# Banded attention and two gated MLPs on one core: VectorE and ScalarE put in written order beside TensorE

## The chip, the cores and the metric

The kernel runs on one core of one Trainium2 chip. The metric is the device time of one execution in microseconds (us); the median of three runs is quoted. One further execution was recorded by the hardware profiler, and every duration below comes from that one.

## What is computed

```python
# attention, for each of 4 sequences and 8 heads: 576 tokens, 64 wide, a window of 128
scores = q @ k.T / 8 + bias               # bias: -slope[h] * |i - j|, masked outside the window
attn = softmax(scores)
x = (attn @ v), heads side by side        # 2304 tokens x 512
# first gated MLP
x = (x @ w_a) * (x @ w_b) @ w_out         # inner width 1536
# second
out = ((x @ w1) * (x @ w2)) @ w3 @ w_out2 # inner width 1024
```

All arrays are float32. The large products are done as three products of a high and a low part in TensorE's fp32r type (`hi` is the rounded value, `lo` the rest).

## The kernel before

**The steps.** Each sequence has five blocks of query rows, four of 128 and one of 64. `RUNS` (line 34) puts them in runs of two, two and one; a step is one run of one pair of heads. Four pairs make 12 steps for a sequence and 48 for the whole, numbered 0 to 47 here; three more steps (`LAG`, line 35) drain the pipeline. `attention_ops` (line 642) yields the calls of each step, and the loop at line 716 makes them.

In step n TensorE does the scores of step n (`scores`, L309), the product with v of step n-3 (`pv`, L395), the transposition of one q or k block of the next run (`prep`, L273), then some work of the first gated MLP, and last the transposition of the probabilities of step n-1 (`probs`, L374). VectorE reduces the scores with their bias to row maxima (`step_exps`, L336), scales the exponentials of step n-1 (`norms`, L349 to L356), and makes the low parts: of the transposed q or k block (`parted`, L283), of the attention output (`pv_out`, L410). ScalarE does the exponentials (L342), the high parts (L282, L409) and most evictions of the transposed probabilities (L376). The small helpers `sub` and `evict` record their own lines, L72, L259 and L261.

**The gate work inside attention.** `Filler` (line 670) holds the work of the first two weight chunks, cut to tiles of 256 tokens: 54 items, each of 12 matmuls, each put down at 1.28 us by its planner. An item is half of a gate product (`g1`, L532) or half of an output product (`g2_two`, L560). At the `None` of every step, `run` is given `FILL` = 1.6 us to spend. An item may go only when its tokens have left attention (`ready`, set at line 412, where the last pair of heads of a run is done) and when the six weight parts are counted as whole.

**The first weights.** `Stages.turn` (line 158) is called once per step (twice in step 1). It moves each of up to three weight parts one stage on, the oldest first, and starts a new one. The stages of `convert` (line 97) turn 64-bit words into float32 and then into a high and a low part: `s0` on ScalarE (L107, L110), `s1` on VectorE (L114, L117, L121), `s3` an add (L126), and `split` (ScalarE makes the high part, L133; a subtraction makes the low part, L72). For the first six parts the add and the subtraction are on VectorE.

**What sets the order.** Line 715 fixes TensorE's order to the order of the program. VectorE's, ScalarE's, GpSimd's and SyncE's orders are chosen at build time by the tile framework from the program order, the dependencies and its own estimate of time. Each engine then runs its list strictly in that order.

**PSUM.** Eight banks: two for the MLP work (`ps_g`), three for scores (`ps_s`, line 182; a step takes two, or one in the short run), three for everything that is transposed and for `pv` (`ps_t`, line 183).

**Warm-up matmuls.** `keep_warm` (line 360) issues matmuls of 512 columns on a dummy tile that nothing reads. `pv` calls it in the first sequence, one after each full block (line 400).

After attention the rest of the gate items runs with more banks, and then the remaining groups of both MLPs (line 750), where TensorE is fed by 512-column matmuls.

Of the kernel before, what the change touches and what calls it, by code (L numbers as in the profile page):

```python
# [8 lines left out]
F32 = mybir.dt.float32  # L9
# [25 lines left out]
LAG = 3  # L35
PES, PTS = 4, 4
FILL = 1.6
PACE = (1.0, 1.0)
TURN = 400
WARM_RUNS, WARM = 3, 1  # L40
# [3 lines left out]
def attention_moe_moe(ctx, tc, q, k, v, w_a, w_b, w_o, w_1, w_2, w_3, w_o2, out):  # L44
# [137 lines left out]
    ps_s = asb.enter_context(tc.tile_pool(name="ps_s", bufs=3, space=PSUM))  # L182
    ps_t = asb.enter_context(tc.tile_pool(name="ps_t", bufs=3, space=PSUM))
# [79 lines left out]
    def prep(run, n):  # L263
# [11 lines left out]
        def parted():  # L275
            ps = hold[0]
            if x == 0 and m == LAST:
                dst = [(slice(j * D, (j + 1) * D), q_t2, slice(j * D, (j + 1) * D)) for j in range(2)]
            else:
                dst = [(slice(0, P), k_t if x else q_t, slice(i * P, i * P + m))]  # L280
            for o, (hi, lo), c in dst:
                nc.scalar.activation(hi[o, :, c], ps[o], ACTF.Copy)  # L282
                sub(nc.vector, lo[o, :, c], ps[o], f32(hi[o, :, c]))  # L283

        return trans, parted
# [30 lines left out]
    def exps(step):  # L316
        run = RUNS[step[1]]
        st = sm_p.tile([P, 4, 2 * len(run)], F32, name="st", bufs=4)
        at = 0
        for i in run:  # L320
            nj = window(i)[3]
            live[step, i]["st"] = st[:, :, at:at + nj]
            step_exps(step, i)
            at += nj
        live[step] = st[:, :, 0:at]

    def step_exps(step, i):
        hp = step[2]
        m, n, nb, nj = window(i)
        d = live[step, i]  # L330
        ps = d.pop("ps")
        pe = d["pe"] = sm_p.tile([P, 2, 2 * P], F32, name="pe", bufs=PES)
        st = d["st"]
        for j in range(nj):
            bias = relb[:, 2 * hp + j, 2 * P - n:] if nj == 2 else relb2[:, hp, :]
            nc.vector.tensor_tensor_reduce(  # L336
                out=pe[:, j, :n], in0=ps[j], in1=bias,
                scale=-1.0 / float(D) ** 0.5, scalar=3.0e38, op0=ALU.add, op1=ALU.min,
                accum_out=st[:, 0, j:j + 1],
            )  # L340
        for j in range(nj):
            nc.scalar.activation(  # L342
                pe[:, j, :n], pe[:, j, :n], ACTF.Exp, bias=st[:, 0, j:j + 1], scale=-1.0,
                accum_out=st[:, 1, j:j + 1],
            )
# [20 lines left out]
    def probs(step, i):  # L366
# [3 lines left out]
        ps = ps_t.tile([P, W], F32, name="tr")[:, 0:nj * n]  # L370
# [4 lines left out]
        t = d["pt"] = sm_p.tile([P, W], F32, name="pt", bufs=PTS)[:, 0:nj * n]  # L375
# [5 lines left out]
    def pv(step):  # L381
# [5 lines left out]
        for i in RUNS[rn]:  # L387
# [12 lines left out]
            if b == 0 and rn < WARM_RUNS and m == P:  # L400
                keep_warm(WARM, warm)

    def pv_out(step):
        b, rn, hp = step
        run = RUNS[rn]
        m = sum(window(i)[0] for i in run)
        o = slice(b * S + run[0] * P, b * S + run[0] * P + m)
        ps = outs.pop(step)[:, :m]
        nc.scalar.activation(x_hi[:, hp, o], ps, ACTF.Copy)  # L409
        sub(nc.vector, x_lo[:, hp, o], ps, f32(x_hi[:, hp, o]))  # L410
        if hp == NP - 1:
            ready[0] = o.stop
# [103 lines left out]
    def g1(g, n, t, tn, zs=range(2), ps=None):  # L516
# [18 lines left out]
        if zs[-1] == 0:  # L535
            return
        gp = pools["gate"]
        a = gp.tile([P, tn], F32, name="a", bufs=pools["abufs"])
        nc.scalar.activation(a, ps[0], ACTF.Copy)  # L539
        gg = gp.tile([P, tn], F32, name="g", bufs=pools["abufs"])  # L540
        nc.vector.tensor_tensor(out=gg, in0=a, in1=ps[1], op=ALU.mult)  # L541
        gh = gp.tile([P, tn], F32R, name="gh", bufs=pools["gbufs"])
        gl = gp.tile([P, tn], F32R, name="gl", bufs=pools["gbufs"])
        nc.scalar.activation(gh, gg, ACTF.Copy)  # L544
        sub(nc.gpsimd, gl, gg, f32(gh))
        gt[g, n, t] = (gh, gl)
# [5 lines left out]
    def g2_two(g, t, m, tn):  # L552
# [10 lines left out]
        nc.scalar.activation(ya, ps, ACTF.Copy)  # L563
# [78 lines left out]
    def attention_ops():  # L642

        late = []
        for n in range(NS + LAG):
            ops, late_1 = late, []
            run, hp = divmod(n, NP)
            if n < NS:
                ops.append(lambda s=steps[n]: scores(s))
                ops.append(lambda s=steps[n]: exps(s))  # L650
            if n >= LAG:
                ops.append(lambda s=steps[n - LAG]: pv(s))
                late_1.append(lambda s=steps[n - LAG]: pv_out(s))
            if hp < len(items(run + 1)):
                f, h = prep(run + 1, hp)
                ops.append(f)
                late_1.append(h)
# [10 lines left out]
        yield B, late  # L668

    class Filler:  # L670


        def __init__(self):
            self.items, self.owed = list(gate_items((0,), cuts(TA), 0)), 0.0

        def run(self, owed):
            self.owed += owed
            while self.owed > 0 and self.items:
# [5 lines left out]
                f()  # L684
# [19 lines left out]
    for x in range(len(items(1))):  # L704
        load_item(1, x)
        f, g = prep(0, x)
        f()
        g()
# [6 lines left out]
    fixed.enter_context(tc.manual_schedule(engines={mybir.EngineType.PE}))  # L715
    for n, (b, ops) in enumerate(attention_ops()):
# [4 lines left out]
        for f in ops:  # L721
            if f is None:
                fl.run(FILL)
            else:
                f()
        paid += PACE[min(b, 1)]
        while n > 0 and paid > 0:
            side.turn()
            paid -= 1
    fixed.close()  # L730
# [8 lines left out]
    for f, _, _ in fl.items:  # L739
        side.turn()  # L740
        f()
# [35 lines left out]
```

## Time and profile before

| | us |
|---|---|
| median of 3 runs (977.60 to 979.57) | 977.85 |
| the profiled execution | 979.18 |
| its span, first to last instruction | 977.40 |
| first scores of attention (step 0) | 8.25 |
| first gate item inside attention (step 11 begins) | 64.24 |
| last step with scores (step 47) begins | 225.44 |
| TensorE matmul busy, whole span | 945.7 (97%) |
| VectorE busy | 520.6 (53%) |
| ScalarE busy | 416.8 (43%) |

The profiled execution took 1.33 us more than the median of the runs; 1.78 us of it lie outside its span. The engines are PE (TensorE's matmuls), PEld (its weight loads), DVE (VectorE), ACT (ScalarE), POOL (GpSimd) and SP (SyncE, which issues the DMAs). Matmuls are pipelined, so the busy time of PE is above the time that it needs; from one group's start to the next group's start is the better measure.

### The profile page before, as it was taken

The page shows a single profiled execution, that of the slowest core. Times are in us where ns is not written, and L with a number is a line of the kernel's source. Part 1 is how long each engine was busy: PE and PEld are TensorE (multiplying, and loading weights), DVE is VectorE, ACT ScalarE, POOL GpSimd, SP SyncE. Part 2 cuts the span into 40 slices and gives each one's busy share as a digit, 9 for nine tenths or more (in the row PEclk, how much of TensorE's full clock was granted, in tenths as well). Part 3 has the DMA queues.
Part 4 walks back from the last instruction along what each step waited for, and adds up shares of the span by engine and source line. Part 5 has one row for each costly group of instructions (what it writes and reads, how often), then busy time and mean ns, then how long its engine had stood idle before and what let it go on. Part 6 is the DMA issues. An engine that isn't in the chain of part 4 may idle for free.

```text
span 977.4 us, 14484 instructions
## 1 busy us (share of the span) xinstructions
PE 945.7 (97%) x5546; PEld 799.0 (82%) x5546; DVE 520.6 (53%) x1177; ACT 416.8 (43%) x951; POOL 341.4 (35%) x285
## 2 busy tenths in 40 slices
PE   6899999989999999999999999999999999999998
PEld 5578988979777888888888888888888888888886
DVE  6968686774998434746563472542541541421322
ACT  5867776775554323543533431442421321311111
POOL 3000000002887223744542462783831631511111
PEclk7799999999999999999999999999999999999999
DMA  9533331202343122413322230210210210000012
GB/s 214 136 71 77 69 69 40 55 1 86 113 127 130 44 87 76 136 70 97 123 72 81 100 110 1 87 44 1 66 64 1 86 44 1 22 1 1 33 65 97
DMA packets 90373, 68.30 MB, mean 70 GB/s; under 512 B 58304, under 2 KB 79296, under 8 KB 90304
## 3 DMA queue, kind: packets, MB, share of 16 engines
q1 hardware_dynamic: 90304, 67.38, 23.9%
q8 instruction: 43, 0.70, 0.3%
q14 instruction: 26, 0.21, 0.1%
HBM read 58.20 MB, written 8.91 MB: 69 GB/s over the span
## 4 chain that ended last, share of the span: by engine, by line
PE 84%; DVE 8%; ACT 3%; DMA 3%; issue 1%; SPq 0%; DVEq 0%; ACTq 0%
PE mm L532 46%; PE mm L571 11%; PE mm L586 10%; PE mm L445 4%; PE tr L395 3%; PE s L309 3%; PE tr L374 2%; PE mm L560 2%; PE tr L273 2%; ACT pe L342 2%; DVE ca L121 1%; DMA raw<-in_moe_w_out 1%; DMA raw<-in_moe_w_b 1%; DVE ca L117 1%; DVE ca L114 1%
## 5 line engine op out<-in xcount | busy, mean ns | idle before, releaser
L72 POOL TENSOR_TENSOR gl<-g,gh 128x512 fp32r<-128x512 f32 (+1 forms) x108 | 123.8, 1147 | 465.6 <-ACT gh L544 465.6
L541 DVE TENSOR_TENSOR g<-a,mm 128x512 f32<-128x512 f32 (+1 forms) x108 | 64.3, 596 | 214.6 <-PE mm L532 191.9
L126 POOL TENSOR_TENSOR ca<-ca,ce 128x512 int32<-128x512 int32 x70 | 91.8, 1312 | 126.7 <-ACT ce L110 66.4
L544 ACT ACTIVATE gh<-g 128x512 fp32r<-128x512 f32 (+1 forms) x108 | 60.3, 558 | 169.7 <-DVE g L541 169.5
L539 ACT ACTIVATE a<-mm 128x512 f32<-128x512 f32 (+1 forms) x108 | 56.0, 519 | 121.6 <-PE mm L532 121.6
L532 PE MATMUL mm<-x_hi,wlA 128*128 128x512 f32 (+1 forms) x464 | 105.9, 349 | 0.0
L532 PE MATMUL mm<-x_lo,whA 128*128 128x512 f32 (+1 forms) x464 | 102.5, 342 | 0.0
L532 PE MATMUL mm<-x_hi,whA 128*128 128x512 f32 (+1 forms) x464 | 101.9, 342 | 0.0
L532 PE MATMUL mm<-x_hi,wlB 128*128 128x512 f32 (+1 forms) x400 | 99.0, 369 | 2.6 <-DVE g L541 2.2
L532 PE MATMUL mm<-x_lo,whB 128*128 128x512 f32 (+1 forms) x400 | 98.4, 368 | 0.0
L532 PE MATMUL mm<-x_hi,whB 128*128 128x512 f32 (+1 forms) x400 | 98.1, 368 | 0.0
L114 DVE TENSOR_SCALAR ca<-ca 128x512 f32<-128x512 f32 x76 | 50.2, 660 | 81.5 <-ACT ca L107 81.5
L532 PEld LDWEIGHTS mm<-x_lo,whA 128*128 128x128 f32 x464 | 76.8, 189 | 10.2
L532 PEld LDWEIGHTS mm<-x_hi,wlA 128*128 128x128 f32 x464 | 76.2, 190 | 11.0 <-issue 1.0
L532 PEld LDWEIGHTS mm<-x_hi,whA 128*128 128x128 f32 x464 | 76.7, 189 | 10.1
L532 PEld LDWEIGHTS mm<-x_hi,wlB 128*128 128x128 f32 x400 | 70.9, 188 | 15.9 <-DVE g L541 2.9
L575 DVE TENSOR_TENSOR acc<-acc,mm 128x512 f32<-128x512 f32 (+1 forms) x100 | 62.1, 630 | 36.8 <-PE mm L571 36.5
L532 PEld LDWEIGHTS mm<-x_lo,whB 128*128 128x128 f32 x400 | 71.1, 189 | 12.6
L107 ACT ACTIVATE ca<-raw 128x512 f32<-128x512 f32 x76 | 50.7, 668 | 71.7 <-DMA raw<-in_moe_w 38.2
L532 PEld LDWEIGHTS mm<-x_hi,whB 128*128 128x128 f32 x400 | 71.0, 189 | 12.5
L121 DVE SCALAR_TENSOR_TENSOR ca<-raw,ca 128x512 int32<-128x512 int32 x76 | 77.9, 1025 | 1.9
L110 ACT ACTIVATE ce<-raw 128x512 int32<-128x512 uint32 x76 | 50.9, 669 | 60.7 <-POOL ca L126 24.3
(113 smaller groups left out, 1698.6 us busy)
## 6 DMA issues: line engine op xcount, KB each, us to landing
raw<-in_moe_w SPq DMA_DIRECT2D x32, 512.0 KB, 3.6
raw<-in_moe_w_out SPq DMA_DIRECT2D x20, 512.0 KB, 3.5
raw<-in_moe_w_a SPq DMA_DIRECT2D x12, 512.0 KB, 3.5
raw<-in_moe_w_b SPq DMA_DIRECT2D x12, 512.0 KB, 3.5
out<-acc SPq DMA_DIRECT2D x18, 256.0 KB, 2.0
raw<-in_q SPq DMA_DIRECT2D x16, 256.0 KB, 2.9
raw<-in_k SPq DMA_DIRECT2D x16, 256.0 KB, 3.9
v<-in_v SPq DMA_DIRECT2D x16, 256.0 KB, 4.0
```

The costliest lines, as they stand in the source:

```text
L72: eng.tensor_tensor(out=out, in0=a, in1=b, op=ALU.subtract)
L110: nc.scalar.activation(e, lw, ACTF.Copy, scale=2.0 ** -29)
L114: nc.vector.tensor_scalar(out=a, in0=a, scalar1=bits(0x38000000), scalar2=None, op0=ALU.max)
L121: nc.vector.scalar_tensor_tensor(out=ai, in0=hw, scalar=-(1 << 30), in1=ai, op0=ALU.bitwise_and, op1=ALU.bitwise_or)
L126: (eng or nc.gpsimd).tensor_tensor(out=ai, in0=ai, in1=es[0], op=ALU.add)
L532: nc.tensor.matmul(p, w[:, z, kk, :], x[:, kk, o], start=(y == 0), stop=(y == len(terms) - 1))
L539: nc.scalar.activation(a, ps[0], ACTF.Copy)
L541: nc.vector.tensor_tensor(out=gg, in0=a, in1=ps[1], op=ALU.mult)
L544: nc.scalar.activation(gh, gg, ACTF.Copy)
L571: nc.tensor.matmul(p, w, x, start=(y == 0), stop=(y == len(terms) - 1))
L575: nc.vector.tensor_tensor(out=ya, in0=ya, in1=p, op=ALU.add)
L586: nc.tensor.matmul(p, x, w, start=(y == 0), stop=(y == len(terms) - 1))
```

## The change

TensorE's, VectorE's and ScalarE's orders are all fixed to the program's inside attention, and the calls of a step are cut into smaller ones and set in a new order. The new order of one step n is: scores (TensorE); the q or k transposition (TensorE); `norms` of step n-1, then `reduce` of step n (VectorE); `pv` of step n-3 (TensorE); the high parts `high` and `pv_high` (ScalarE); loads; the gate items (TensorE), before them the high and low parts of the gate product of the step before; `low` (VectorE); the exponentials (ScalarE); the transposition of the probabilities `turned` of step n-1 (TensorE); `pv_low` and the eviction of block 0 (VectorE); the gate's first copy and the other evictions (ScalarE); the gate product (VectorE); and last `Stages.turn`.

`FILL` falls from 1.6 to 1.47. The score banks fall from three to two, the `ps_t` banks rise from three to four. In `convert` the second ScalarE operation (L110) moves from the first stage to the second. The warm-up matmuls leave `pv`; in their place `Filler.run` issues six in every step until the first gate item has gone.

```diff
-FILL = 1.6
+FILL = 1.47
...
-WARM_RUNS, WARM = 3, 1
+WARM = 6
...
         def s0():
 
             nc.scalar.activation(a, f32(hw), ACTF.Abs)
+
+        def s1():
+
             e = pools["conv"].tile([P, W], I32, name="ce", bufs=1)
             es.append(e)
             nc.scalar.activation(e, lw, ACTF.Copy, scale=2.0 ** -29)
-
-        def s1():
-
...
-    ps_s = asb.enter_context(tc.tile_pool(name="ps_s", bufs=3, space=PSUM))
-    ps_t = asb.enter_context(tc.tile_pool(name="ps_t", bufs=3, space=PSUM))
+    ps_s = asb.enter_context(tc.tile_pool(name="ps_s", bufs=2, space=PSUM))
+    ps_t = asb.enter_context(tc.tile_pool(name="ps_t", bufs=4, space=PSUM))
...
-            if b == 0 and rn < WARM_RUNS and m == P:
-                keep_warm(WARM, warm)
...
+            if now:
+                ops.append(lambda s=now: scores(s))
+            ops.append(trans)
+            if last:
+                ops.append(lambda s=last: norms(s))
+            if now:
+                ops.append(lambda s=now: reduce(s))
+            if old:
+                ops.append(lambda s=old: pv(s))
+            ops.append(high)
+            if old:
+                ops.append(lambda s=old: pv_high(s))
...
             ops.append(None)
-            if 1 <= n <= NS:
-                ops.append(lambda s=steps[n - 1]: norms(s))
-                ops += [lambda s=steps[n - 1], i=i: probs(s, i) for i in RUNS[steps[n - 1][1]]]
-            late = late_1
+            ops.append(low)
+            if now:
+                ops.append(lambda s=now: exps(s))
+            if last:
+                ops += [lambda s=last, i=i: turned(s, i) for i in RUNS[last[1]]]
+            if old:
+                ops.append(lambda s=old: pv_low(s))
+            if last:
+                ops += [lambda s=last, i=i: taken(s, i) for i in RUNS[last[1]] if i == 0]
+            ops.append(0)
+            if last:
+                ops += [lambda s=last, i=i: taken(s, i) for i in RUNS[last[1]] if i]
+            ops.append(1)
...
         def run(self, owed):
+            self.finish(2)
             self.owed += owed
...
-                f()
+                self.fresh = False
+                for x, g in enumerate(f()):
+                    self.rest[x].append(g)
+            if self.fresh:
+                keep_warm(WARM, warm)
...
-    fixed.enter_context(tc.manual_schedule(engines={mybir.EngineType.PE}))
+    fixed.enter_context(tc.manual_schedule(engines={mybir.EngineType.PE, mybir.EngineType.DVE, mybir.EngineType.Activation}))
...
             if f is None:
                 fl.run(FILL)
+            elif isinstance(f, int):
+                fl.finish(f)
```

## Rows read from the trace of the kernel before

**Rows 1.** The page, part 1: busy time of TensorE over the span.
```profile
PE 945.7 (97%) x5546; PEld 799.0 (82%) x5546; DVE 520.6 (53%) x1177; ACT 416.8 (43%) x951; POOL 341.4 (35%) x285
```
**Rows 2.** Windows: stretch, its us, busy us (instructions) of each engine, granted clock, DMA.
```profile
12.32:21.24 8.92, 3.95 (x23) 3.35 (x22) 7.27 (x29) 5.74 (x17) 0.00 (x0) 0.50 1.27 251
21.24:53.79 32.55, 28.17 (x205) 19.28 (x205) 31.39 (x113) 25.15 (x74) 0.00 (x0) 0.74 0.57 131
53.79:64.24 10.45, 9.25 (x91) 6.82 (x89) 7.61 (x31) 8.04 (x24) 0.00 (x0) 1.00 0.25 56
...
139.53:153.99 14.46, 10.76 (x104) 8.28 (x104) 11.60 (x52) 11.01 (x38) 0.73 (x1) 0.88 0.26 59
...
195.06:208.00 12.94, 9.40 (x103) 7.16 (x102) 11.56 (x52) 11.12 (x38) 0.73 (x1) 1.00 0.00 0
```
**Rows 3.** TensorE's timeline, step 25, with one gate item: start us, us, instruction.
```profile
126.99 0.33 PE L309 MATMUL s<-k_th,q_tl 64*128 64x128 f32 x2
...
128.82 0.48 PE L560 MATMUL mm<-gh,wlA 128*128 128x256 f32 x2
...
130.34 0.82 PE L374 MATMUL tr<-ident,pe 128*128 128x128 f32 x6
131.09 0.33 PE L309 MATMUL s<-k_th,q_tl 64*128 64x128 f32 x2
```
**Rows 4.** TensorE's timeline, step 28, without a gate item.
```profile
139.53 0.39 PE L309 MATMUL s<-k_th,q_tl 64*128 64x256 f32 x2
...
140.43 0.88 PE L395 MATMUL tr<-pt,v 128*64 128x128 f32 x12
141.24 0.46 PE L273 MATMUL tr<-ident,raw 64*128 64x64 f32 x4
141.63 0.44 PE L374 MATMUL tr<-ident,pe 128*128 128x128 f32 x2
143.63 0.77 PE L374 MATMUL tr<-ident,pe 128*128 128x128 f32 x4 [1.56 <-DVE pt L261]
```
**Rows 5.** TensorE's timeline, step 1: the transposition that waits for its load.
```profile
18.95 1.09 PE L273 MATMUL tr<-ident,raw 128*128 128x128 f32 x4 [4.97 <-DMA raw<-in_k]
19.83 1.49 PE L374 MATMUL tr<-ident,pe 128*128 128x128 f32 x6
```
**Rows 6.** VectorE's groups, 12.32 to 64.24 us: busy us, mean ns of one, idle before.
```profile
L336 DVE CUSTOM_DVE_ANT_0 pe<-s,relb 128x256 f32<-128x256 f32 x25 | 9.6, 421 | 0.5 <-PE s L309 0.5
L356 DVE TENSOR_SCALAR pe<-pe,st 128x256 f32<-128x256 f32 x27 | 8.1, 350 | 0.2
...
L72 DVE TENSOR_TENSOR x_lo<-tr,x_hi 128x256 fp32r<-128x256 f32 x8 | 3.4, 423 | 1.8 <-ACT x_hi L409 1.6
...
L72 DVE TENSOR_TENSOR q_tl<-tr,q_th 128x512 fp32r<-128x512 f32 x3 | 2.1, 689 | 0.5 <-ACT q_th L282 0.4
...
L350 DVE RECIPROCAL st<-st 128x4 f32<-128x4 f32 x8 | 1.4, 174 | 0.1
```
**Rows 7.** ScalarE's groups, 12.32 to 64.24 us.
```profile
L342 ACT ACTIVATE pe<-pe,st 128x256 f32<-128x256 f32 x26 | 12.9, 497 | 1.3 <-DVE st L336 1.2
L259 ACT ACTIVATE pt<-tr 128x512 f32<-128x512 f32 x12 | 6.7, 587 | 0.0
...
L110 ACT ACTIVATE ce<-raw 128x512 int32<-128x512 uint32 x6 | 4.0, 675 | 1.6 <-DVE ca L126 1.4
...
L133 ACT ACTIVATE whA<-ca 128x512 fp32r<-128x512 f32 x6 | 3.8, 626 | 3.4 <-DVE ca L126 3.4
```
**Rows 8.** TensorE's groups, 0 to 64.24 us: the warm-up matmuls inside attention.
```profile
L364 PE MATMUL mm<-warm 128*128 128x512 f16 x16 | 7.3, 458 | 0.0
```
**Rows 9.** Windows along the granted clock, first, second and last of five at 0.50.
```profile
10.92:24.58 13.66, 8.30 (x46) 7.18 (x47) 11.28 (x45) 8.74 (x27) 0.00 (x0) 0.50 1.29 238
...
31.40:41.64 10.24, 10.11 (x58) 5.83 (x56) 10.15 (x38) 7.79 (x20) 0.00 (x0) 0.50 0.46 130
...
154.28:157.70 3.42, 3.42 (x30) 2.87 (x28) 2.61 (x12) 1.96 (x8) 0.00 (x0) 0.50 0.02 5
```

More of the change, by code (lines that the diff above doesn't have):

```diff
@@ L273, in trans, with parts, high, low @@
                 nc.tensor.transpose(ps[:, hp, :], t[0:m, hp * P:(hp + 1) * P], ident[0:m, 0:m])
-        def parted():
-            ps = hold[0]
+        def parts():
             if x == 0 and m == LAST:
[L278 to L285, printed above, removed]
+                return [(slice(j * D, (j + 1) * D), q_t2, slice(j * D, (j + 1) * D)) for j in range(2)]
+            return [(slice(0, P), k_t if x else q_t, slice(i * P, i * P + m))]
+        def high():
+            for o, (hi, lo), c in parts():
+                nc.scalar.activation(hi[o, :, c], hold[0][o], ACTF.Copy)
+        def low():
+            for o, (hi, lo), c in parts():
+                sub(nc.vector, lo[o, :, c], hold[0][o], f32(hi[o, :, c]))
+        return trans, high, low
     live = {}
@@ L369, in probs @@
         pe = d.pop("pe")
-        ps = ps_t.tile([P, W], F32, name="tr")[:, 0:nj * n]
+        ps = d["ps"] = ps_t.tile([P, W], F32, name="tr")[:, 0:nj * n]
         for j in range(nj):
@@ L535, in g1, with first, product, parted @@
         if zs[-1] == 0:
[L536 to L546, printed above, removed]
+            return []
+        gp, r = pools["gate"], []
+        def first():
+            a = gp.tile([P, tn], F32, name="a", bufs=pools["abufs"])
+            nc.scalar.activation(a, ps[0], ACTF.Copy)
+            r.append(a)
+        def product():
+            gg = gp.tile([P, tn], F32, name="g", bufs=pools["abufs"])
+            nc.vector.tensor_tensor(out=gg, in0=r[0], in1=ps[1], op=ALU.mult)
+            r.append(gg)
+        def parted():
+            gg = r[1]
+            gh = gp.tile([P, tn], F32R, name="gh", bufs=pools["gbufs"])
+            gl = gp.tile([P, tn], F32R, name="gl", bufs=pools["gbufs"])
+            nc.scalar.activation(gh, gg, ACTF.Copy)
+            sub(nc.gpsimd, gl, gg, f32(gh))
+            gt[g, n, t] = (gh, gl)
+        if g:
+            first()
+            product()
+            parted()
+        return [first, product, parted]
     def at_acc(t):
@@ L642, in attention_ops @@
     def attention_ops():
-        late = []
         for n in range(NS + LAG):
-            ops, late_1 = late, []
+            ops = []
             run, hp = divmod(n, NP)
[L648 to L653, printed above, removed]
-            if hp < len(items(run + 1)):
-                f, h = prep(run + 1, hp)
-                ops.append(f)
-                late_1.append(h)
+            now = steps[n] if n < NS else None
+            last = steps[n - 1] if 1 <= n <= NS else None
+            old = steps[n - LAG] if n >= LAG else None
+            trans = high = low = lambda: None
+            if hp < len(items(run + 1)):
+                trans, high, low = prep(run + 1, hp)
+            if now:
[10 more added lines that the diff above has]
+                ops.append(lambda s=old: pv_high(s))
             if run + 1 < NR and hp < len(blocks_of(run + 1)[1]):
@@ L674, in __init__, with finish @@
             self.items, self.owed = list(gate_items((0,), cuts(TA), 0)), 0.0
+            self.rest, self.fresh = [[], [], []], True
+        def finish(self, x):
+            for f in self.rest[x]:
+                f()
+            self.rest[x] = []
         def run(self, owed):
+            self.finish(2)
             self.owed += owed
@@ L705, in attention_moe_moe @@
         load_item(1, x)
-        f, g = prep(0, x)
-        f()
-        g()
+        for f in prep(0, x):
+            f()
     side.parts += weight_parts(0)
@@ L729, in attention_moe_moe @@
             paid -= 1
+    for x in range(3):
+        fl.finish(x)
     fixed.close()
@@ L740, in attention_moe_moe @@
         side.turn()
-        f()
+        for g in f():
+            g()
     side.parts += weight_parts(1)
```

74 lines of the change are left out of this document (38 added, 36 removed).

## The prediction, made before the change was run

> **What bounds the kernel now.** I began with the page: TensorE is busy for 97% of the span [rows 1], so time is won only where TensorE stands still or is slowed. The windows by stage say where that is [rows 2]. From the start of step 1 at 12.32 us to the first gate item at 64.24 us the bound is VectorE: it is busy for 7.27 + 31.39 + 7.61 = 46.3 of 51.9 us, because six weight parts are converted on it beside the attention steps, and TensorE waits for it. From 64.24 on TensorE is the bound. A step with one gate item takes 4.10 us, and its groups follow one another without a wait; the item itself is 1.52 us, from 128.82 to 130.34 [rows 3]. The exceptions are steps 28 to 30 and 40 to 42, in which no gate item is due. They take 14.46 and 12.94 us for three steps each [rows 2]. Of such a step TensorE needs 0.90 us for scores, 0.81 for the product with v, 0.39 for the transposed block [rows 4] and 0.75 for the probabilities [rows 3], 2.85 in all and 8.55 for three. The rest is waiting, for example 1.56 us for a bank that VectorE has still to empty [rows 4]. Behind attention nothing is changed: the same 14 gate items are left over under both values of `FILL`, by my count of the planner's loop, so I move that part as a block with the end of attention. All that matters is how much earlier or later step 47 begins (225.44 us before).
>
> **Part 1: the fill rate and the fixed order from step 11 on.** One sequence brings 2.25 tiles of 6 items, 13.5 items of 1.28 us by the planner, or 17.3 us for 12 steps. At 1.6 us a step the planner spends 19.2 and runs dry; at 1.47 it spends 17.6. Going through the loop with the due times gives steps 28 to 30 and 40 to 42 without an item at 1.6, which the trace confirms, and 29, 30 and 40 to 42 at 1.47. So five dry steps are left of six, and the largest burst falls from three items to two. The dry steps cost 14.46 - 8.55 = 5.9 and 12.94 - 8.55 = 4.4 us above TensorE's need [rows 2, 4], and the low clock just behind the first of them slows 3.42 us of work by half, 1.7 us [rows 9]: 12.0 us that could be had. A dry step can't be shorter than VectorE's work in it, 11.60 / 3 = 3.9 us [rows 2], against 2.85 for TensorE, so each of the five keeps 1.0 us: 5.0. I take a gain of 12.0 - 5.0 = **7.0 us**. The ends are 12.0 (VectorE gets ahead across steps) and 2 (the written orders add waits of their own in the steps that now have none).
>
> **Part 2: the written order in the first steps.** What the planner did before, and the program's order can't do, is to let VectorE convert weights while attention waits for a load. In step 1 the transposition on TensorE waits until 18.95 us for k [rows 5], and VectorE worked for 7.27 of the 8.92 us around it [rows 2]. In the new order ScalarE's head is then `high` of step 1, with the exponentials of step 1 behind it, and VectorE's head is `low` of step 1, with an eviction and the first conversion stage behind it. The transposition ends at about 20.0 us, `high` (about 0.6 us) at 20.6. By then VectorE has done `low` of step 0, `norms` of step 0 and `reduce` of step 1, some 3.4 us (0.69 for the 512-column low part, the rest at 0.28 to 0.42 an instruction [rows 6]). Of its 46.3 us, 42.9 are left; without another wait that is 63.5 us.
>
> Then it waits. First for the eviction of step 0's probabilities: their transposition stands on TensorE behind six warm-up matmuls, 1.3 us at full clock and 2.6 at half, and itself takes 0.75 to 1.5 [rows 3, 5]; VectorE's `low` covers 0.6 of it: **2 us** (0.8 to 3.5). Second, for each weight part, in steps 3, 4, 5, 7, 8 and 9 by the stage count. The subtraction (L72) needs ScalarE's high part (L133), and that stands behind the step's exponentials and evictions. In a step of a run of two full windows VectorE takes 0.34 + 4 x 0.30 = 1.5 us for `norms` and 4 x 0.38 = 1.5 for `reduce`, then 0.84 for the two low parts: 3.9 us, and stands at the subtraction. ScalarE gets its first exponential at 1.96 us, takes 4 x 0.50, then two evictions of 0.56 and the high part of 0.63: 5.7 us [rows 6, 7]. That is a wait of 1.8 us, in steps 5 and 7. In steps 3 and 4, with one eviction on ScalarE, the same sum gives 0.7; in 8, 1.2; in 9, 0.4: together **6.6 us** (0 if ScalarE's work always overlaps, 11 if every part costs 1.8). What queues behind is all the rest of VectorE's step, `norms` of the next one first, for which TensorE's probabilities wait. Moving L110 one stage on costs its 0.67 us either way [rows 7]; it lies on ScalarE beside VectorE's stage, and I price it at nothing while VectorE is the bound, at 6 x 0.67 = 4 us if ScalarE were.
>
> The warm-up matmuls rise from 16 to 66, six in each of steps 0 to 10. The 16 took 7.3 us [rows 8]; 50 more are 11 us at the full clock and 22.9 at the measured mean of 458 ns. In steps 0 to 8 they stand in TensorE's wait for VectorE and cost nothing more; if that cover were missing they would cost all of it. In steps 9 and 10 VectorE has little left to do, and TensorE becomes the bound at about 3.5 us a step against some 2.5 of VectorE: **2.1 us**. The sum is 63.5 + 2 + 6.6 + 2.1 = 74.2 us; step 11 begins at about 74 in place of 64.24, **9.8 us later**. The ends are 65 (no waits but the tail) and 79 (all at their upper bounds).
>
> **Part 3: the banks.** With two score banks step n+1's scores need all of `reduce` of step n, not three quarters of it. One `reduce` is 0.38 us [rows 6], 48 x 0.38 = 18 us if it always decided. But some 3 us of TensorE's own work lie between [rows 3], so I take 0. The fourth `ps_t` bank removes the wait for L261 [rows 4]; it is in the 12.0 us of part 1 already.
>
> **The sum** is 9.8 - 7.0 = +2.8 us. The profiled execution (979.18) would become 982.0; it stands 1.33 us above the median of the runs, so for the median I say 977.85 + 2.8, about **980.7 us**.
>
> **The rivals.**
> *The first steps cost little, faster.* The waits of part 2 shrink if k's load lands earlier (SyncE's order is still the planner's) or if ScalarE is ahead of VectorE. At 65 to 69 us for step 11 and a gain of 7 to 12 behind it, the result is 967 to 976 us, say 971. For it speaks that VectorE's work alone needs no more than 63.5 us; against it that each wait follows from a list that is run strictly in order.
>
> *The clock decides, faster.* TensorE runs at 0.50 of its clock, 1.2 of 2.4 GHz, in five stretches of attention, 13.66 + 10.24 + 3.41 + 3.42 + 3.42 = 34.2 us [rows 9]. If TensorE were the bound there and the six warm-up matmuls held it at 2.4, half of that would come back: 977.85 - 17 = 961 us. The Trainium skill has this as a rule (TensorE: Matmul & The Clock Gate, Terms): the penalty is about the throttled time times the share of pulses withheld, which is the same 17 us. The trace speaks against it: in the stretch from 31.40 VectorE is busy for 10.15 of 10.24 us [rows 9], so a faster TensorE would only wait longer, and the one stretch where the clock cost TensorE's own time is in part 1. So I go by the row, and give it 0.04.
>
> *No net change.* Parts 1 and 2 cancel within 0.2%, or the planner's orders of before were near the written ones already: 976 to 980 us.
>
> *The written order also stalls the steady steps, slower by more.* The gate product on VectorE is the last of a step and waits for ScalarE's copy, which stands behind the exponentials; `norms` of the next step waits behind it, and TensorE's probabilities for that. It decides once the product comes later than TensorE's 3.3 us of work between two groups of probabilities [rows 3] allow. At 0.3 us in each of 35 steps it takes 10 us: 991 us.
>
> **How the numbers follow.** A difference of 0.2%, 2 us, is about what a measurement of this kernel tells from none. The forecast case, a startup loss that outweighs the steady gain, spans 980 to 986 and has 0.38; the steady stalls (986 to 993) have 0.10; no net change 0.22; the cheap first steps 0.26; the clock 0.04. Faster by over 0.2% is 0.30, within 0.22, slower 0.48. The ends of the terms give 977.85 + 0.8 - 12 = 966.6 and 977.85 + 14.8 - 2 = 990.6; the range that holds 8 in 10 is 968 to 988. As the chances lie on both sides, the forecast case's own range of 980 to 986 stands beside it.
>
> **What would show it.** The first gate matmul (L532 now) of attention stands at about 74 us, not at 64. VectorE's list of waits has the weight part's subtraction behind ScalarE's high part with some 6 us, and `low` behind `high` with 3 to 5 us at the start. L364 counts 66 matmuls of 512 columns. Steps 29, 30 and 40 to 42 have no gate item, and take about 4 us. From the first gate item to step 47 it takes about 154 us, not 161. A first gate item before 69 us proves part 2 wrong; a steady stretch above 159 us proves part 1 wrong; a change in the time from step 47 to the end would break the assumption that the rest moves as a block.

## The result and the profile after

The changed kernel took **988.75 us** (median of 4 runs, 988.27 to 989.57) against 978.0 for the kernel before on the same chip: a ratio of **1.0106 (95% interval 1.0094 to 1.0118)**, 10.75 us slower. The forecast of 980.7 had the sign right and the size wrong, and the time lies above the range of 968 to 988. The profiled execution took 988.4 us with a span of 986.6, 9.2 more than the span of before; the other 1.5 us of the medians' difference is how the two profiled executions stand to their medians (1.2 above before's in these runs, 0.35 below after's).

The page, part 1, of after, is nearly the line of before [rows 1], and tells nothing of where the time went:

```profile
PE 955.2 (97%) x5596; PEld 802.2 (81%) x5596; DVE 519.8 (53%) x1177; ACT 416.1 (42%) x951; POOL 343.3 (35%) x285
```

The windows tell it: stretch, its us, busy us (instructions) of PE, PEld, DVE, ACT, POOL, granted clock, DMA share, GB/s. The first begins at the time of [rows 2]; the cuts are the starts of steps 11 and 47.

```profile
12.32:76.25 63.93, 50.46 (x362) 33.66 (x361) 47.64 (x167) 40.76 (x119) 0.00 (x0) 0.87 0.52 115
76.25:233.20 156.95, 153.97 (x1539) 135.80 (x1538) 112.60 (x489) 115.33 (x370) 9.63 (x13) 1.00 0.24 53
233.20:986.60 753.40, 743.71 (x3658) 627.66 (x3656) 353.92 (x505) 256.25 (x459) 325.23 (x255) 1.00 0.21 67
```

| stretch | before | after | difference | forecast |
|---|---|---|---|---|
| up to step 11, the first gate item | 64.24 | 76.25 | +12.0 | +9.8 |
| step 11 to step 47 | 161.20 | 156.95 | -4.25 | -7.0 |
| step 47 to the end of the span | 751.97 | 753.42 | +1.45 | 0 |

In the first stretch VectorE is busy for 47.64 of 63.93 us and stands still for 16.3; before it was busy for 46.3 of 51.9 [rows 2]. Its list of waits, 8 to 77 us (what waited for what, us in total, times, longest), accounts for most of that; its five longest:

```profile
DVE wlA L72 <- ACT whA L133: 7.5, 6, 2.3
DVE k_tl L72 <- ACT k_th L282: 3.8, 2, 3.3
DVE pt L261 <- PE tr L375: 1.7, 1, 1.7
DVE ca L114 <- ACT ca L107: 1.2, 1, 1.2
DVE q_tl L72 <- ACT q_th L282: 1.1, 1, 1.1
```

The largest is the subtraction of each of the six weight parts, behind ScalarE's high part. Two timelines, VectorE's and then ScalarE's, show the third of the six. It belongs to the calls of step 5, though TensorE has begun step 6 at 47.49:

```profile
48.03 0.42 DVE L72 TENSOR_TENSOR x_lo<-tr,x_hi 128x256 fp32r<-128x256 f32 x1
50.37 0.69 DVE L72 TENSOR_TENSOR wlA<-ca,whA 128x512 fp32r<-128x512 f32 x1 [1.93 <-ACT whA L133]
50.98 0.42 DVE L114 TENSOR_SCALAR ca<-ca 128x512 f32<-128x512 f32 x1
51.43 0.43 DVE L117 TENSOR_SCALAR ca<-ca 128x512 int32<-128x512 int32 x1
```

```profile
48.27 0.49 ACT L343 ACTIVATE pe<-pe,st 128x256 f32<-128x256 f32 x1
...
48.76 1.05 ACT L259 ACTIVATE pt<-tr 128x512 f32<-128x512 f32 x2
49.72 0.62 ACT L133 ACTIVATE whA<-ca 128x512 fp32r<-128x512 f32 x1
```

The order is the one the prediction wrote down: the last exponential, two evictions, then the high part; VectorE has run out of work at 48.4 and takes the subtraction 1.93 us later.

In step 1 the load of k is late, as before [rows 5]. TensorE's timeline, then VectorE's:

```profile
18.93 0.83 PE L273 MATMUL tr<-ident,raw 128*128 128x128 f32 x4 [3.15 <-DMA raw<-in_k]
19.55 2.77 PE L365 MATMUL mm<-warm 128*128 128x512 f16 x6
22.11 1.07 PE L375 MATMUL tr<-ident,pe 128*128 128x128 f32 x6
```

```profile
20.43 0.69 DVE L72 TENSOR_TENSOR k_tl<-tr,k_th 128x512 fp32r<-128x512 f32 x1 [3.31 <-ACT k_th L282]
22.78 0.42 DVE L261 COPY pt<-tr 128x256 f32<-128x256 f32 x1 [1.67 <-PE tr L375]
24.41 0.43 DVE L114 TENSOR_SCALAR ca<-ca 128x512 f32<-128x512 f32 x1 [1.21 <-ACT ca L107]
```

VectorE stands 3.31 us for k, then 1.67 for an eviction whose transposition has six warm-up matmuls in front of it, and only then takes up the weights.

### The profile page after: what moved, and what is told of

The parts are those of the page before. It is cut to its first block, busy times and chain, and to the rows that moved or that the text cites. A ratio compares the mean times of both kernels' runs of the same rounds, so it can differ in the third digit from the quotient of the medians.

```text
span 986.6 us, 14620 instructions
## 1 busy us (share of the span) xinstructions
PE 955.2 (97%) x5596; PEld 802.2 (81%) x5596; DVE 519.8 (53%) x1177; ACT 416.1 (42%) x951; POOL 343.3 (35%) x285
## 4 chain that ended last, share of the span: by engine, by line
PE 85%; DVE 6%; ACT 3%; issue 2%; DMA 2%; SPq 1%; POOL 1%; POOLq 0%; ACTq 0%; DVEq 0%
PE mm L539 47%; PE mm L593 12%; PE mm L608 10%; PE mm L452 4%; PE tr L399 3%; PE s L312 3%; PE tr L375 2%; PE mm L582 2%; PE tr L273 2%; ACT pe L343 1%; DVE ca L121 1%; DVE pe L357 1%; SPq L242 1%; DVE ca L117 1%; DMA raw<-in_moe_w_out 1%
## 5 line engine op out<-in xcount | busy, mean ns | idle before, releaser
L114 DVE TENSOR_SCALAR ca<-ca 128x512 f32<-128x512 f32 x76 | 51.9, 683 | 92.6 <-ACT ca L107 92.5
```

The source lines that it names most:

```text
L114: nc.vector.tensor_scalar(out=a, in0=a, scalar1=bits(0x38000000), scalar2=None, op0=ALU.max)
```

## The experiments

Each is given by its edit against the changed kernel, unless it says "before". Step numbers and stretches are those of the table above. The ratio is to the kernel before, with its 95% interval; both were timed on the same chip. The median of before lies between 977.5 and 979.5 us from chip to chip, so two experiments are compared by their ratios or by their profiles.

**Planner's order for VectorE and ScalarE.** All else as in the changed kernel.

```diff
-manual_schedule(engines={mybir.EngineType.PE, mybir.EngineType.DVE, mybir.EngineType.Activation})
+manual_schedule(engines={mybir.EngineType.PE})
```

> The changed kernel with only TensorE's order fixed; VectorE's and ScalarE's are the planner's again, all else (1.47, two and four banks, six warm-up matmuls, the new sequence of calls) as changed. My theory: the late start of the gate work (76.25 us against 64.24) comes from VectorE and ScalarE run in written order beside the weight conversion, so it goes: first gate item at 64 to 67 us, the waits of the low-part subtraction for ScalarE's high part (7.5 us in six) under 3 us, total 974 to 979. Rival, warm-up matmuls or the two score banks: the first gate item stays at 72 or later and the total at 985 or more.

Measured: 978.36 us, 1.0002 [0.9993, 1.0012]. Step 11 begins at 66.42 (9.83 earlier than in the changed kernel), the stretch from 11 to 47 takes 156.1, the rest 752.83. VectorE's waits up to step 11 hold no line for `wlA`:

```profile
DVE pe L331 <- PE s L312: 3.1, 4, 0.9
DVE st L350 <- ACT pe L343: 2.1, 3, 1.0
DVE ca L114 <- ACT ca L107: 1.2, 1, 1.2
DVE k_tl L72 <- ACT k_th L282: 0.8, 2, 0.6
```

And where the written order stood still from 17.1 to 20.4, VectorE's timeline is full of weight stages:

```profile
18.34 0.42 DVE L114 TENSOR_SCALAR ca<-ca 128x512 f32<-128x512 f32 x1
18.68 0.69 DVE L126 CUSTOM_DVE_ANT_0 ca<-ca,ce 128x1024 uint16<-128x1024 uint16 x1
19.28 0.42 DVE L117 TENSOR_SCALAR ca<-ca 128x512 int32<-128x512 int32 x1
...
19.74 0.69 DVE L121 SCALAR_TENSOR_TENSOR ca<-raw,ca 128x512 int32<-128x512 int32 x1
```

So the two written orders cost 10.4 us by the medians. By the profiles it is 11.3: 9.8 ahead of step 11, 0.85 from step 11 to step 47 and 0.6 behind it, so they win nothing in the steady steps. The other 2.2 of the 12.0 us that step 11 lost stay with the planner's orders; they belong to the rest of the change (calls, banks, warm-ups, L110), which this run does not take apart.

**The high part a stage earlier.** The stage `split` is cut in two, for the first six parts: the high part in one turn, the subtraction in the next (with the count that says the part is there).

```diff
-        return [s0, s1, s3, lambda: split(a, hi, lo, eng)]
+        if eng is None:
+            return [s0, s1, s3, lambda: split(a, hi, lo, eng)]
+        return [
+            s0, s1, s3,
+            lambda: nc.scalar.activation(hi, a, ACTF.Copy),
+            lambda: sub(eng, lo, a, f32(hi)),
+        ]
...
-                return convert(raw, hi, lo, eng=None if g else nc.vector) + [count]
+                st = convert(raw, hi, lo, eng=None if g else nc.vector)
+                if g:
+                    return st + [count]
+                return st[:-1] + [lambda: (st[-1](), count())]
```

> The changed kernel with the last conversion stage cut in two: ScalarE makes the high part in one turn, VectorE subtracts in the next, a step later, and the part is counted whole in that same turn, so the gate work still begins in step 11. Moving the call from the end of a step to the start of the next had left both engines' lists as they were; this edit changes their order. My theory: the six waits of the subtraction (7.5 us) fall under 1.5, and as VectorE is the bound the first gate item comes 4 to 7 us earlier, at 69 to 72 us; total 982 to 985. Rival, VectorE only meets the next wait: step 11 at 74 or later, total 987 or more.

Measured: 981.66 us, 1.0023 [1.0011, 1.0035]. Step 11 begins at 68.47, 7.8 us earlier. The waits of the subtraction, 7.5 us, are gone from VectorE's list, and its first lines are now these (the edit moves the line numbers by 6):

```profile
DVE k_tl L72 <- ACT k_th L288: 3.9, 3, 3.4
DVE pt L267 <- PE tr L381: 1.3, 1, 1.3
```

The gain equals the wait that was taken away, within 0.3 us: VectorE is the bound there, and what it stands still moves the start of the gate work by as much. Step 11 and the median both came a little better than I had expected.

**The planner in steps 0 and 1 only**, the written orders from step 2 on.

```diff
-    fixed.enter_context(tc.manual_schedule(engines={mybir.EngineType.PE, mybir.EngineType.DVE, mybir.EngineType.Activation}))
+    fixed.enter_context(tc.manual_schedule(engines={mybir.EngineType.PE}))
...
+        if n == 2:
+            fixed.close()
+            fixed.enter_context(tc.manual_schedule(engines={mybir.EngineType.PE, mybir.EngineType.DVE, mybir.EngineType.Activation}))
```

> The changed kernel with VectorE's and ScalarE's orders left to the planner in steps 0 and 1 and fixed from step 2 on. My theory, the wait for the load of k (VectorE 3.3 us, and 2.9 us for the eviction and the first stage behind it) is the other part of the loss: the first gate item comes 2 to 5 us earlier, at 71 to 74 us, total 984 to 987. Rival, the two steps cost nothing, as step 2 begins at 23.12 us in place of 21.24 only: the first gate item at 75.5 or later, total 988 or more.

Measured: 986.42 us, 1.0077 [1.0059, 1.0094]; step 11 begins at 74.08, 2.2 us earlier.

```profile
DVE wlA L72 <- ACT whA L133: 7.4, 6, 2.4
...
DVE k_tl L72 <- ACT k_th L282: 1.4, 2, 1.2
```

The wait behind k falls by 2.4 us, to the 1.4 shown, and those of the weights stay at 7.4: the two are separate costs.

**One warm-up matmul a step in place of six.**

```diff
-WARM = 6
+WARM = 1
```

> The changed kernel with one warm-up matmul per step in place of six (11 in place of 66). My theory: VectorE is the bound in steps 2 to 8, so only steps 9 and 10, where TensorE is, gain: first gate item 1 to 3 us earlier (73 to 75 us), total 986 to 988. Rival, the warm-up matmuls stand before the probabilities and set the pace: first gate item at 68 or earlier, total under 983. Rival, they hold the clock up and pay for themselves: granted clock lower in the first 76 us and the total 990 or more.

Measured: 986.81 us, 1.0098 [1.0083, 1.0113], an interval that overlaps the changed kernel's; step 11 begins at 74.61, 1.64 us earlier. Only 0.5 us of that lie in steps 9 and 10, where I had placed it (7.22 us for the two in place of 7.71). By the start of step 2 it is 1.7 us ahead (21.42 in place of 23.12), and step 2 gives 0.5 of that back: VectorE's wait of 1.7 us for the eviction in step 1 is gone from its list. The warm-up line of the changed kernel (all of them, ns min/median/max; ten of 256 columns precede attention):

```profile
L365 PE MATMUL mm<-warm x76: 379/379/634, 2.8 to 75.9; 128*128 128x512 f16 x66, 128*128 128x256 f16 x10
```

This run also tests the rival in which the clock decides. The last line of two answers of windows sums the five stretches at 0.50 of the clock up to step 11, first in the changed kernel, then with one warm-up:

```profile
sum 17.03, PE 16.87 PEld 11.68 DVE 11.51 ACT 11.34 POOL 0.00; mean PE 3.37 PEld 2.34 DVE 2.30 ACT 2.27 POOL 0.00
```

```profile
sum 34.09, PE 26.46 PEld 21.49 DVE 25.52 ACT 20.74 POOL 0.00; mean PE 5.29 PEld 4.30 DVE 5.10 ACT 4.15 POOL 0.00
```

The six matmuls do hold the clock up: 17 us at 1.2 GHz in place of 34 with one. Yet with 34 the gate work starts no later, but 1.64 us earlier. By the rule of the Trainium skill (TensorE: Matmul & The Clock Gate, Terms), that the penalty is about the throttled time times the share of pulses withheld, I estimate a loss of 8.5 us for the other 17. The trace does not agree: step 11 came earlier, and VectorE is the bound of that stretch.

**Three banks for scores and three for the rest, as before.**

```diff
-    ps_s = asb.enter_context(tc.tile_pool(name="ps_s", bufs=2, space=PSUM))
-    ps_t = asb.enter_context(tc.tile_pool(name="ps_t", bufs=4, space=PSUM))
+    ps_s = asb.enter_context(tc.tile_pool(name="ps_s", bufs=3, space=PSUM))
+    ps_t = asb.enter_context(tc.tile_pool(name="ps_t", bufs=3, space=PSUM))
```

> The changed kernel with three score banks and three banks for transposed data, as before. My theory: the banks decide nothing in the first steps (first gate item within 1 us of 76.25) and the stretch from there to step 47 (156.95 us) grows by 0 to 5 us as the probabilities wait for a bank; total 988 to 994. Rival, two score banks hold the scores back: the total falls by 2 us or more.

Measured: 992.57 us, 1.0157 [1.0136, 1.0178]. By the spans it is 4.6 us slower than the changed kernel: 2.1 ahead of step 11 (78.38), which I had not expected, 2.2 in the stretch from 11 to 47 (159.17) and 0.3 behind it. TensorE's waits in that stretch are of another kind than the changed kernel's, and sum to 4.4 us in place of 3.0:

```profile
PE tr L375 <- DVE k_tl L72: 2.6, 3, 1.6
PE tr L375 <- DVE q_lastl L72: 1.8, 2, 1.7
```

The transposed probabilities need a bank that the q or k block holds until `low` has read it, and VectorE reaches `low` only behind `norms` and `reduce` of the step. So in the new order two and four banks are better than three and three. The run changes both pools at once, and the same split was not tried in the kernel before.

**The q or k transposition behind the product with v.** TensorE's order in a steady step is new as well: the transposition now stands between scores and `pv`.

```diff
             if now:
                 ops.append(lambda s=now: scores(s))
-            ops.append(trans)
...
             if old:
                 ops.append(lambda s=old: pv(s))
+            ops.append(trans)
```

> The changed kernel with the q or k transposition put behind the product with v, where it stood before, in place of ahead of it. The trace of the changed kernel shows the group of four 128-column transpositions taking 0.58 us up to the product with v that follows, against 0.41 up to a gate item before. If that is a cost of the neighbourhood on TensorE, the steps of the first two blocks fall from 4.27 to about 4.09 us, the stretch from the first gate item to step 47 from 156.95 to 153.5 to 155.5 us, total 985.5 to 987.5. Rival, it is a wait for something else that moves with it: steps stay at 4.27 and the total within 1 us of 988.75.

Measured: 989.26 us, 1.0119 [1.0104, 1.0134], no different from the changed kernel: neither the gain that I expected nor the unchanged steps of the rival came out. TensorE's timeline of step 25 in the changed kernel, then of the same step here:

```profile
137.68 0.66 PE L273 MATMUL tr<-ident,raw 128*128 128x128 f32 x4
138.27 0.60 PE L399 MATMUL tr<-pt,v 128*64 128x64 f32 x8
138.79 0.74 PE L539 MATMUL mm<-x_hi,wlA 128*128 128x256 f32 x4
```

```profile
137.46 0.60 PE L399 MATMUL tr<-pt,v 128*64 128x64 f32 x8
137.99 0.65 PE L273 MATMUL tr<-ident,raw 128*128 128x128 f32 x4
138.40 0.72 PE L539 MATMUL mm<-x_hi,wlA 128*128 128x256 f32 x4
```

From its start to the next group's the transposition takes 0.59 us in front of `pv` and 0.41 in front of a gate item. Of the first four steps of the three later sequences, twelve in all, eleven get shorter by 0.18 to 0.20 us, for example from 4.27 to 4.08. Yet steps 16, 17 and 28 grow by 0.13 to 0.14 each, and steps 29, 30 and 41, without an item, grow from 3.53, 4.04 and 4.56 to 4.31, 4.61 and 5.42, so that the stretch from 11 to 47 is 156.78 against 156.95. What TensorE saves in a full step, it loses in the next dry ones.

**The stage turns at the start of the next step** in place of the end of this one. Nothing of VectorE's or ScalarE's stands between the two places, so both lists keep their order; I saw that only behind the run.

```diff
+        while n > 1 and paid > 0:
+            side.turn()
+            paid -= 1
         for f in ops:
...
-        while n > 0 and paid > 0:
-            side.turn()
-            paid -= 1
```

> The changed kernel, all three orders fixed, with the call of the conversion stages moved from the end of a step to the start of the next, so that ScalarE's high part of a weight stands ahead of that step's exponentials and evictions. My theory, the subtraction's wait for the high part is a matter of what stands ahead of it in ScalarE's list: the six waits of 7.5 us fall under 3 us and the first gate item comes at 69 to 73 us in place of 76.25, total 982 to 986. Rival, the load of k in step 1 alone makes the loss: the first gate item stays at 75 or later, total 987 or more. Rival, any written order costs about the same, the stalls move elsewhere on VectorE: 75 us or later with the high-part wait gone.

Measured: 989.39 us, 1.0112 [1.0093, 1.013], step 11 at 75.81, and 7.3 us of waits for the high part. My expectation was wrong, and the run tells no theory from another; it only shows how little such a kernel moves when its orders don't.

**The planner up to step 11, all three orders written from there.**

```diff
-    fixed.enter_context(tc.manual_schedule(engines={mybir.EngineType.PE, mybir.EngineType.DVE, mybir.EngineType.Activation}))
+    fixed.enter_context(tc.manual_schedule(engines={mybir.EngineType.PE}))
...
             acc_half(1)
+            fixed.close()
+            fixed.enter_context(tc.manual_schedule(engines={mybir.EngineType.PE, mybir.EngineType.DVE, mybir.EngineType.Activation}))
```

> The changed kernel with TensorE's order alone fixed in steps 0 to 10 and all three from step 11 on. My theory: the first gate item at 65 to 69 us as with the planner's order, the stretch behind it 155 to 158 us as in the changed kernel, total 976 to 980, level with the planner's orders. Rival, written order gains behind step 11 and only the start hid it: total under 975.

Measured: 977.9 us, 0.9995 [0.9986, 1.0004], level with the planner throughout (1.0002). The stretch from 11 to 47 takes 159.61 us, outside what I expected. But here TensorE only puts out step 11's scores early, at 64.02; the first gate matmul stands at 68.15, against 67.92 with the planner throughout. From step 12 to step 47 it takes 152.19 us, against 152.18 in the changed kernel and 151.32 with the planner. The written orders of the steady steps bring no gain that can be measured.

**The fill rate alone, in the kernel before.**

```diff
-FILL = 1.6
+FILL = 1.47
```

> The kernel before with 1.47 in place of 1.6, nothing else. My theory: all of the steady stretch's gain comes from the rate, none from the orders: from step 11 to step 47 155 to 158 us in place of 161.2, step 11 at 64.24, total 972 to 975 and so better than both. Rival, the gain needs the written orders or the fourth bank: within 2 us of 978.

Measured: 975.81 us, 0.997 [0.9959, 0.9981]. The stretch from 11 to 47 takes 156.7 us, what it takes in the changed kernel: the whole steady gain is the rate's. The median is a little above what I expected.

```profile
64.49:221.19 156.70, 152.39 (x1539) 135.72 (x1538) 115.37 (x489) 115.87 (x369) 9.72 (x13) 0.99 0.25 54
```

**The kernel before with one item in every step.** At the planner's own 1.28 us no step from 11 on runs dry.

```diff
-FILL = 1.6
+FILL = 1.28
```

> The kernel before with 1.28 in place of 1.6, the planner's own price of one item, so that the loop gives one item in each step from 12 to 46 and no dry step before step 50. My theory, dry steps are bound by VectorE and are the whole loss: from step 11 to step 47 149 to 153 us with about three items fewer in it (they follow at full speed), total 966 to 972. Rival, the items put off collide with the stage behind attention: the rest from step 47 to the end grows by more than 6 us and the total is 973 or more.

Measured: **967.53 us, 0.9889 [0.9875, 0.9904]**. The stretch:

```profile
64.28:210.93 146.65, 146.20 (x1503) 130.46 (x1502) 115.41 (x489) 113.88 (x367) 9.83 (x13) 1.00 0.26 58
```

It takes 14.55 us less than before, more than I expected. Three items fewer have gone by step 47 (its 36 matmuls fewer than at 1.47, or 4.6 us at the 1.52 us of [rows 3]), and the rest takes 3.3 us longer; what is left is the waiting of the dry steps, about 10 us.

**The changed kernel with that rate.**

```diff
-FILL = 1.47
+FILL = 1.28
```

> The changed kernel with 1.28 in place of 1.47. The kernel before gained 14.55 us from step 11 to step 47 by that rate (146.65 against 161.2). If the rate's effect does not depend on the orders, the stretch falls from 156.95 to 147 to 151 us, the rest behind step 47 grows by about 3.5 us, total 983 to 986. Rival, the written orders lose more when every step is at TensorE's pace: stretch 153 or more, total 988 or more.

Measured: 985.33 us, 1.0063 [1.0042, 1.0084]. The stretch from 11 to 47 falls to 147.29, step 11 stays late at 77.69, and the rest takes 760.5 in place of 753.4, twice the growth that I expected. Three items moved behind step 47 are 4.6 of those 7.1 us; the cause of the other 2.5 stays open.

**Everything that was found put together**: the planner up to step 11, the written orders from there, 1.28, one warm-up, the transposition behind `pv`.

```diff
-FILL = 1.47
+FILL = 1.28
...
-WARM = 6
+WARM = 1
...
-            ops.append(trans)
...
                 ops.append(lambda s=old: pv(s))
+            ops.append(trans)
...
-    fixed.enter_context(tc.manual_schedule(engines={mybir.EngineType.PE, mybir.EngineType.DVE, mybir.EngineType.Activation}))
+    fixed.enter_context(tc.manual_schedule(engines={mybir.EngineType.PE}))
...
             acc_half(1)
+            fixed.close()
+            fixed.enter_context(tc.manual_schedule(engines={mybir.EngineType.PE, mybir.EngineType.DVE, mybir.EngineType.Activation}))
```

> From step 11 on all three orders fixed, before it TensorE's alone; 1.28; the transposition behind the product with v; one warm-up matmul per step; two and four banks. Against the kernel before with 1.28 alone (967.5) this shows what the written orders and the banks are worth where TensorE is the bound. My theory, nothing, since no VectorE or ScalarE wait ends a steady step there: 965 to 970. Rival, the steps of the longer runs, 4.4 to 4.6 us in that kernel, fall to TensorE's 4.1 to 4.4: under 965.

Measured: 966.97 us, 0.9888 [0.986, 0.9916], level with the one-number edit of before. Step 47 begins 3.6 us earlier than there (207.33 against 210.93), of which 2.5 are won before step 12, and the rest takes 3.1 us longer. The first gate matmul stands at 63.26, 4.9 us earlier than with the planner up to step 11 and six warm-ups (68.15). Up to there the two kernels differ in the warm-ups and in the place of the transposition alone, and with the written orders that place did not bring step 11 forward (76.90 against 76.25). This points to the six warm-ups as the source of the 2.2 us that stayed with the planner's orders, without showing it.

## Why the prediction was wrong in size

**What bounds which stretch held.** VectorE is the bound up to step 11 (taking 7.5 us of its waits away brought 7.8), TensorE after it, but for the dry steps.

**Part 2, the written order in the first steps, was right in mechanism and 2.2 us short.** Term by term:

| term | forecast | measured |
|---|---|---|
| k's low part begins, VectorE's work done by then | 20.6, 3.4 us done | 20.43, 3.25 us done |
| VectorE's work from there to step 11 | 42.9 | 44.39 |
| eviction behind the warm-ups | 2 | 1.7 |
| six subtractions behind the high part | 6.6 | 7.5 |
| wait for ScalarE's first copy of a weight | no term | 1.2 |
| warm-ups in steps 9 and 10 | 2.1 | 0.5 (run with one) |
| step 11 begins | 74.2 | 76.25 |

The six waits of the subtraction came near the table of the prediction: 0.77, 0.55, 1.93, 2.25, 1.22 and 0.76 us for its 0.7, 0.7, 1.8, 1.8, 1.2 and 0.4. What failed is the size of two terms and the lack of a third: VectorE's work after k's low part (1.5 us more), the subtractions (0.9 more) and the wait for the first copy (1.2); the warm-ups, of which too much was expected, hide part of it. The measured terms without the warm-ups, which come from another run, sum to 75.2, and VectorE's gaps of less than 0.15 us make up the rest. The prediction took VectorE's work from the windows of before, as if it did not depend on the order. It does: in the written order an instruction often stands right behind the one whose result it needs. The same 28 instructions up to step 11 (six of L114, six of L117, sixteen small ones of `norms`) hold VectorE for 7.8 us in place of 6.3 in before and with the planner's orders, from the start of each to the next start or to its own end. In VectorE's timeline of the third part above, L117 starts 0.45 us behind L114, after its end (50.98 and 51.43). Before, an independent instruction followed, 0.31 us behind:

```profile
18.67 0.40 DVE L114 TENSOR_SCALAR ca<-ca 128x512 f32<-128x512 f32 x1
18.98 0.69 DVE L126 CUSTOM_DVE_ANT_0 ca<-ca,ce 128x1024 uint16<-128x1024 uint16 x1
```

**Part 1 failed by its size: a gain of 4.25 where I took 7.0.** I measured each step from 11 to 46 against the shortest step at the same place of the sequence in the two kernels with before's calls (before, and the rate alone), with 1.44 us for an item, and the steps of the last run, which transpose no further block, by themselves. Before stands 11.6 us above that, near the 12.0 that "could be had"; after stands 7.3 above, not 5.0. Of these, 4.3 us are in the five dry steps, where I had 5.0: steps 29, 30 and 40 to 42 take 3.53, 4.04, 2.84, 4.56 and 4.05 us. The other 3.0 had no term: 1.9 for the moved transposition (0.19 us in twelve steps, less 0.14 in three), 0.7 in the two steps with a burst behind a dry run, and 0.5 in small amounts. But adding these terms would have been luck. The kernel with the transposition moved back has 6.5 us in the dry steps and 7.2 in all; the rate alone has 6.7 and 7.1. So the five dry steps cost about 1.3 us each in both, and the total is the same in all three kernels: the step of the prediction that fails is "each of the five keeps 1.0 us". It took VectorE's work in a dry step, 3.9 us, as the least that the step can last. Single steps undercut that: step 40 here, and in the kernel before step 18, a seventh step without an item that the prediction overlooked (97.14 to 99.88, 2.74 us). In a row of dry steps the changed kernel's trace shows more than VectorE's work, a loop through two engines. Its rows are the starts of `norms` on VectorE in the calls of steps 41 to 43, then the first exponentials of steps 41 and 42 on ScalarE:

```profile
208.72 0.17 DVE L350 TENSOR_SCALAR st<-st 128x4 f32<-128x4 f32 x1
...
212.77 0.17 DVE L350 TENSOR_SCALAR st<-st 128x4 f32<-128x4 f32 x1 [0.45 <-ACT pe L343]
...
216.82 0.17 DVE L350 TENSOR_SCALAR st<-st 128x4 f32<-128x4 f32 x1 [0.78 <-ACT pe L343]
```

```profile
210.66 0.51 ACT L343 ACTIVATE pe<-pe,st 128x256 f32<-128x256 f32 x1 [0.95 <-DVE st L331]
...
214.71 0.51 ACT L343 ACTIVATE pe<-pe,st 128x256 f32<-128x256 f32 x1 [0.74 <-DVE st L331]
```

`norms` waits for the last exponential, and the first exponential for the first reduction, which the written order puts behind `norms`: a turn takes 4.05 us, 1.2 above TensorE's 2.85. This is read from the trace; no run with another order of the two tests it, and what sets the dry steps under the planner's orders stays open.

**Part 3, the banks, was priced at 0 beside part 1.** With three and three the changed kernel is 4.6 us slower by the spans, 2.1 of it ahead of step 11, where the prediction gave the banks no part. The wait that I named for two score banks, scores behind `reduce`, comes to 2.2 us in the stretch from 11 to 47, nearly all of it in the dry steps, and not to 0.

**The rest as a block failed by 1.45 us.** TensorE's timeline shortly after attention, and the windows' line of the stretch that follows, with its granted clock of 0.50:

```profile
298.58 0.79 PE L593 MATMUL mm<-gh,wlB 128*128 128x512 f32 x2 [1.79 <-DVE acc L597]
```

```profile
299.10:302.50 3.40, 3.40 (x9) 2.64 (x9) 2.95 (x6) 2.04 (x5) 1.78 (x2) 0.50 0.42 147
```

Before has neither the 1.79 us wait nor the low clock there; it had other waits. But the low clock does not explain the 1.45 us: the kernels with one warm-up and with the early stage turns have no low clock there, and take 753.46 and 753.41 for this part. With the rate alone it takes 751.75, as before (751.97); with the new order of calls 752.46 to 753.8 in every kernel at 1.47. Why the new order costs 0.5 to 1.9 us behind attention stays open.

**The rivals.** No net change and the cheap first steps fall with step 11 at 76.25. The rival of the clock falls with the run of one warm-up. The steady stalls named nearly the right time, 991, for a wrong reason: TensorE's waits from 11 to 47 sum to 3.0 us where before has 7.2, and the steady stretch became shorter. The upper end of the range was 0.75 us too low: the misses of the three stretches, 2.2 + 2.75 + 1.45 = 6.4 us, all lie on one side, and 2.8 + 6.4 makes the 9.2 of the spans. So the direction came out for the reason given, and the size failed in three terms: the written order's start (12.0 for 9.8), the dry steps (a gain of 4.25 for 7.0) and the part behind step 47 (1.45 for 0).

## What to carry to other kernels

Before an engine's order is written out, ask in the stretch where that engine is the bound what stands behind each wait that the order fixes: two halves of one job on two engines, issued together, make the second engine wait for the first one's whole queue, and issuing the first half a stage earlier takes the wait away (step 11 came 7.8 us earlier here). A change of many parts should be taken apart before it is kept: this one's only gain over the kernel before was a number, and the same number turned further was worth 11 us with nothing else touched. Where a filler runs dry, try first the rate at which it never does; in this kernel that was worth more than a shorter step, whose gain the next dry steps took back.

## What the runs showed of the hardware that I had not expected

A group of four transpositions of 128 columns takes 0.59 us of TensorE's time, from its start to the next group's, when the product with v (64 columns wide) follows it and 0.41 when a gate item of 256 columns does, with no wait in either (step 25 of two runs): what this group costs depends on its neighbour. And 17 us more at half clock made no loss that could be seen while VectorE was the bound: with 34 us of it the gate work began 1.64 us earlier than with 17.
